# Parking a lane pair's results feature-major in DRAM, transposing them a quarter per unit in the next pair, and issuing the sync queue in hand-set order

## Chip, cores, metric

One core of one Trainium2 chip. The metric is the device time of the kernel in microseconds (us). All runs are single-core. A run is called "slow" when it is over 1.5% above the fastest run of the same kernel; ratios use the other ("fast") runs.

## The reference

A cross network of six layers on 16384 rows of 1024 features, all bf16:

```python
def reference(x0, ws, bs):          # x0 [16384,1024], ws [6,1024,1024], bs [6,1024]
    x = x0
    for l in range(6):
        proj = jnp.einsum('bd,de->be', x, ws[l]) + bs[l]
        x = x0 * proj + x
    return x
```

## The kernel before

The batch is cut into 8 *pairs* (`lp`) of two *lanes* of 1024 rows. Features lie on partitions, so an input is transposed on the way in and a result on the way out. A *unit* is one layer of one lane. Each 1024x1024 product is done by two levels of a seven-product scheme: TensorE runs a unit's 20 steps (`idx` 0 to 19), ScalarE (ACT) moves the sums out of PSUM, VectorE (DVE) adds them, multiplies by `x0` and adds `x`. All weights come back from DRAM (`Lc`) for each layer, nine loads of 512 KB per two units, through a ring of ten buffers: `wp<-Lc` in the profile. The parts that matter (`# ...` marks a cut):

```python
x0L = [res.tile([P, 2, KD, NB], BF16, ...) for i in range(2)]   # x0 of each lane, resident
xL  = [res.tile([P, 2, KD, NB], BF16, ...) for i in range(2)]   # x of each lane, resident
# ...
def pre_x0(lp, lane, eh, n):        # x0 of the next pair: transposed, then put aside in DRAM
    xs = late["xf"].tile([P, KH, KH, P], BF16, name="xf")            # two buffers
    nc.sync.dma_start_transpose(out=xs[:]..., in_=x0[r0:r0 + NB, eh * H:(eh + 1) * H])
    nc.sync.dma_start(x0s[lp % 2, lane, eh, n], xs[:]...)
def fetch_x0(lp, lane, eh, n):      # ... and fetched when the lane changes pairs
    nc.sync.dma_start(q(x0L[lane], eh, n)..., x0s[lp % 2, lane, eh, n])
def store_quarter(lp, lane, eh, n, xf):
    nc.sync.dma_start_transpose(out=dst, in_=xf[:]...)               # SBUF -> SBUF, into xL
    nc.sync.dma_start(out[r0:r0 + NB, ...], q(xL[lane], eh, n)...)
# ... in a unit:
P1s, Q2, U2s, S53, U3s, P5s = (ev_pool.tile(...) ...)                # bufs=1
def x_out(c, eh, n):                # c is Q2 (n = 0) or S53 (n = 1)
    if last_layer:
        xf = late["xf"].tile(...)
        tt(xf[:]..., c..., q(xst, eh, n)..., ADD)
        store_quarter(lp, lane, eh, n, xf)
    elif l > 0:
        nc.gpsimd.dma_start(q(xst, eh, n), c, accum_op=ADD)          # DMA that adds: xL += c
    else:
        tt(q(xst, eh, n), c, q(x0T, eh, n), ADD)
```

In layers 1 to 4 half of each unit's update is added by DMA from Q2 and S53 (`xL<-Q`, `xL<-S` on the POOL queue). I call these the Q and the S accumulate. In layer 5 VectorE adds into an `xf` buffer that is transposed and stored; in layer 0 VectorE adds as well. The scheduler decides the order of the sync queue (SP); the other engines follow program order.

## Time and profile before

| | |
|---|---|
| median of runs | 2375.8 us (2372.7 to 2377.8) |
| span of the profiled run | 2373.7 us |
| TensorE busy | 2264.8 us |
| one unit in the middle of a pair | 23.38 us |
| twelve such units | 280.6 us |
| pair to pair, five periods from 596.8 to 2058.5 | 292.3 us on average |

The page, lines of parts 1 and 2. Each digit is the busy share, or the clock granted to TensorE, of one fortieth of the span.

```profile
span 2373.7 us, 32873 instructions
PE 2264.8 (95%) x12659; PEld 1267.6 (53%) x12912; DVE 2114.4 (89%) x2096; ACT 1784.9 (75%) x2485; POOL 110.7 (5%) x133
...
PE   5999999999899998999989999999998999989996
...
PEclk9999999999999999999999999999999999999998
DMA  9876599546994579845798457975579656865566
```

TensorE dips every fifth digit or so, at the pair boundaries, where the DMA engines are full; between them the DMA share drops to 4 or 5 tenths. One boundary in the timeline of TensorE (start, duration, instruction; in brackets the idle time before it and what ended it):

```profile
617.23 0.60 PE L281 MATMUL XB<-t,wp 128*128 128x256 bf16 x4
622.41 1.04 PE L281 MATMUL XB<-ti,wp 128*128 128x256 bf16 x4 [4.59 <-DMA wp<-Lc]
623.24 1.91 PE L269 MATMUL XA<-t,wp 128*128 128x512 bf16 x4
...
628.68 1.03 PE L269 MATMUL XA<-x0L,wp 128*128 128x512 bf16 x4
```

TensorE waits 4.59 us for a weight load, and afterwards four matmuls take 1.91 us where they normally take 1.03. The windows of the same stretch (columns: window, its length, busy us and count of PE, PEld, DVE, ACT, POOL, granted clock, DMA share, GB/s; a packet's whole time is booked in the window in which it starts, so a share can pass 1):

```profile
616.00:620.00 4.00, 1.83 (x11) 0.81 (x9) 0.00 (x0) 1.17 (x3) 0.00 (x0) 1.00 1.17 250
620.00:624.00 4.00, 1.59 (x6) 0.89 (x7) 3.40 (x5) 0.51 (x1) 0.00 (x0) 0.55 0.91 320
624.00:628.00 4.00, 3.98 (x15) 1.95 (x15) 2.44 (x2) 2.20 (x3) 0.00 (x0) 0.60 1.04 404
628.00:632.00 4.00, 3.97 (x22) 2.13 (x22) 3.80 (x5) 3.15 (x5) 0.00 (x0) 1.00 1.20 252
```

Why the load is late shows in the timeline of the sync queue (here the duration is that of the issue):

```profile
611.74 0.98 SPq L171 DMA_DIRECT2D x0L<-x0s  x1
612.82 5.47 SPq L176 DMA_TRANSPOSE xL<-xf  x1
618.39 1.01 SPq L110 DMA_DIRECT2D wp<-Lc  x2
```

The two loads stand behind a transpose that holds the queue for 5.47 us. From the view of waits (total us, times, longest):

```profile
DVE xf L65 <- DMA xL<-xf: 59.5, 15, 6.3
PE XB L281 <- DMA wp<-Lc: 33.6, 13, 4.7
DVE t L65 <- DMA xL<-S: 28.5, 23, 2.4
...
ACT S L261 <- DMA xL<-S: 4.5, 6, 1.3
```

So the kernel is bound by TensorE's issue inside a pair, and loses 11 to 12 us (292.3 - 280.6) at each of seven boundaries.

### The profile page before, as it was taken

Reading aid. Unit: us, or ns where it says so; the run is one execution under the profiler, and the core shown is the slowest. Engines: PE = TensorE matmul, PEld = TensorE weight load, DVE = VectorE, ACT = ScalarE, POOL = GpSimd, SP = SyncE. Lnnn points to the kernel's source line nnn. Section 1 sums busy time; section 2 is a strip of 40 time slices with the busy share of each in tenths; the row PEclk is TensorE's granted clock in tenths of the full one; section 3 lists DMA queues with packets and bytes.
Section 4 is the critical chain, followed back from the end, with each engine's and each line's share of the span. In section 5 each row is a group of like instructions: output and inputs, shape, how many; then the busy total and the mean of one; then the engine's idle time right before and its main releaser. Section 6 shows DMA issues by size and latency. Waiting matters only on the chain.

```text
span 2373.7 us, 32873 instructions
## 1 busy us (share of the span) xinstructions
PE 2264.8 (95%) x12659; PEld 1267.6 (53%) x12912; DVE 2114.4 (89%) x2096; ACT 1784.9 (75%) x2485; POOL 110.7 (5%) x133
## 2 busy tenths in 40 slices
PE   5999999999899998999989999999998999989996
PEld 2555545555455554555545555555554555545553
DVE  5999879999898988999889998899988999889987
ACT  3777777777677776777867777677776777768775
POOL 0000000000000000000000000000000000000000
PEclk9999999999999999999999999999999999999998
DMA  9876599546994579845798457975579656865566
GB/s 274 236 231 216 159 285 252 156 126 179 290 254 128 134 189 291 247 121 138 189 300 229 124 150 201 299 202 133 156 208 303 183 140 167 219 187 133 150 171 142
DMA packets 410236, 468.27 MB, mean 197 GB/s; under 512 B 278496, under 2 KB 324064, under 8 KB 410080
## 3 DMA queue, kind: packets, MB, share of 16 engines
q1 hardware_dynamic: 391648, 399.05, 57.2%
q0 software_dynamic: 18432, 67.12, 14.8%
q8 instruction: 101, 1.65, 0.3%
q14 instruction: 55, 0.45, 0.1%
HBM read 240.65 MB, written 91.23 MB: 140 GB/s over the span
## 4 chain that ended last, share of the span: by engine, by line
PE 75%; DVE 15%; DMA 6%; issue 2%; ACT 1%; SPq 1%; DVEq 0%; ACTq 0%; POOLq 0%
PE pA L269 34%; PE XA L269 22%; PE XB L281 18%; DVE t L65 4%; DMA xL<-xf 4%; DVE D L65 3%; DVE ti L65 3%; DVE S L65 2%; DMA x0L<-x0s 1%; DVE xL L65 1%; DVE Q L65 1%; DVE xf L65 1%; SPq L161 0%; DMA xL<-S 0%; DMA wp<-Lc 0%
## 5 line engine op out<-in xcount | busy, mean ns | idle before, releaser
L269 PEld LDWEIGHTS <-wp 128*128 128x128 bf16 x7712 | 757.3, 98 | 757.0 <-issue 35.1
L269 PE MATMUL pA<-t,wp 128*128 128x512 bf16 x2982 | 758.7, 381 | 6.4
L281 PEld LDWEIGHTS <-wp 128*128 128x128 bf16 x5040 | 494.6, 98 | 311.2 <-DMA wp<-Lc 42.5
L261 ACT CAST F<-XB 128x1024 bf16<-128x1024 f32 x360 | 364.3, 1012 | 262.9 <-PE XB L281 256.5
L281 PE MATMUL XB<-ti,wp 128*128 128x256 bf16 x2880 | 435.1, 274 | 43.0 <-DMA wp<-Lc 33.2
L269 PE MATMUL XA<-t,wp 128*128 128x512 bf16 x1474 | 386.1, 385 | 3.7 <-DMA wp<-Lc 0.5
L269 PE MATMUL XA<-xL,wp 128*128 128x512 bf16 x1256 | 325.5, 379 | 4.0 <-ACT P5s L261 2.6
L269 PE MATMUL pA<-xL,wp 128*128 128x512 bf16 x1254 | 323.2, 379 | 1.3
L264 ACT ACTIVATE U3s<-pA,b_all 128x512 bf16<-128x512 f32 x384 | 264.4, 689 | 39.0 <-PE pA L269 19.0
L261 ACT CAST G<-XB 128x512 bf16<-128x512 f32 x360 | 212.0, 589 | 97.1 <-PE XB L281 95.8
L264 ACT ACTIVATE P1s<-pA,b_all 128x512 bf16<-128x512 f32 x384 | 266.4, 694 | 24.2 <-PE pA L269 16.5
L264 ACT ACTIVATE U2s<-pA,b_all 128x512 bf16<-128x512 f32 x384 | 266.5, 694 | 12.7 <-PE pA L269 4.2
L261 ACT CAST S<-XA 128x1024 bf16<-128x1024 f32 x192 | 194.3, 1012 | 66.6 <-PE XA L269 61.0
L65 DVE TENSOR_TENSOR D<-D,x0L 128x4096 bf16<-128x4096 bf16 x96 | 220.0, 2292 | 13.6 <-ACT D L264 10.1
L261 ACT CAST P5s<-XA 128x1024 bf16<-128x1024 f32 x192 | 195.1, 1016 | 44.4 <-DVE D L65 27.2
L65 DVE TENSOR_TENSOR t<-xL 128x4096 bf16<-128x4096 bf16 x80 | 183.4, 2293 | 41.6 <-DMA xL<-S 28.5
L65 DVE TENSOR_TENSOR t<-xL,t 128x2048 bf16<-128x2048 bf16 x160 | 194.9, 1218 | 0.0
L65 DVE TENSOR_TENSOR xL<-D,xL 128x4096 bf16<-128x4096 bf16 x64 | 146.7, 2292 | 7.0 <-DVE D L65 0.5
L327 POOL DMA_DIRECT2D xL<-Q x64 | 55.2, 862 | 1870.7 <-ACT U3s L264 948.5
L281 PE MATMUL XB<-t,wp 128*128 128x256 bf16 x1008 | 139.8, 276 | 0.0
L65 DVE TENSOR_TENSOR S<-S,U2s 128x2048 bf16<-128x2048 bf16 x96 | 117.2, 1221 | 24.0 <-ACT S L261 24.0
L65 DVE TENSOR_TENSOR Q<-Q,P1s 128x2048 bf16<-128x2048 bf16 x96 | 117.6, 1225 | 19.7 <-ACT Q L261 10.9
(43 smaller groups left out, 1744.0 us busy)
## 6 DMA issues: line engine op xcount, KB each, us to landing
wp<-Lc SPq DMA_DIRECT2D x378, 512.0 KB, 4.9
xL<-Q POOLq DMA_DIRECT2D x64, 512.0 KB, 6.2
xL<-S POOLq DMA_DIRECT2D x64, 512.0 KB, 6.8
out_dram<-xL SPq DMA_DIRECT2D x64, 512.0 KB, 4.1
x0s<-xf SPq DMA_DIRECT2D x56, 512.0 KB, 3.4
x0L<-x0s SPq DMA_DIRECT2D x56, 512.0 KB, 6.3
Lc<-wp SPq DMA_DIRECT2D x48, 512.0 KB, 4.7
wp<-in_ws_dram SPq DMA_DIRECT2D x13, 512.0 KB, 6.7
```

Source lines behind the costliest of these rows:

```text
L65: return nc.vector.tensor_tensor(out=out, in0=in0, in1=in1, op=op)
L261: nc.scalar.copy(out=dst, in_=src)
L264: nc.scalar.activation(out=dst, in_=src, func=IDENT, bias=bias_col(eh, m), scale=1.0)
L269: nc.tensor.matmul(dst, lhsT=w_[:, k, m * P:(m + 1) * P], rhs=b_[:, k, :], start=(start and k == 0), stop=(k == KH - 1), skip_group_check= ...
L281: nc.tensor.matmul(dst[:, m * NQ:(m + 1) * NQ], lhsT=wv[:, k, m * P:(m + 1) * P], rhs=b_[:, k, :], start=(start and m == 0 and k == 0), st ...
L327: nc.gpsimd.dma_start(q(xst, eh, n), c, accum_op=ADD)
```

## The change

Its intent is to take the output transposes out of the boundary. In layer 5 of all pairs but the last, results go into `xL` by the ordinary path (accumulates and one add), are *parked* as they are in DRAM (`outs`), and one quarter per unit is transposed and stored during layers 1 to 4 of the next pair, beside one quarter of the next x0. From the second pair on the sync queue is in program order, and `at(u, step, ...)` puts each transfer at a step of a unit. The diff, cut to its core:

```diff
+    def park_out(lp, lane, eh, n):
+        nc.sync.dma_start(outs[...].rearrange("(k r) b -> r k b", r=P), q(xL[lane], eh, n))
+    def post_out(lp, lane, eh, n):
+        xs = late["xf"].tile([P, KH, KH, P], BF16, name="xf")
+        nc.sync.dma_start_transpose(out=xs[:]..., in_=outs[lp % 2, lane, eh, n])
+        return lambda: nc.sync.dma_start(out[r0:r0 + NB, ...], xs[:]...)
...
+        if lp == 1 and sp_order is None:
+            sp_order = ctx.enter_context(tc.manual_schedule(engines={nc.sync.engine}))
...
-            if last_layer:
+            if direct:                       # last layer of the last pair only
...
                 nc.gpsimd.dma_start(q(xst, eh, n), c, accum_op=ADD)
+                if last_layer:
+                    at(u + n, 17 if n == 0 else 3, lambda: park_out(lp, lane, eh, n))
...
-        if 1 <= l <= 4 and lp + 1 < NLP:
-            pre_x0(lp + 1, i_ // 4, i_ % 2, (i_ // 2) % 2)
+        if 1 <= l <= 4:
+            if lp > 0:
+                at(u, 1, lambda u=u, a_=(lp - 1,) + qt: at(u, 7, post_out(*a_)))
+            if lp + 1 < NLP:
+                at(u, 9, lambda u=u, a_=(lp + 1,) + qt: at(u, 17, pre_x0(*a_)))
...
-                    fetch_x0(lp + 1, lane, 1, n)
+                    at(u + 1, 6, lambda n=n: fetch_x0(lp + 1, lane, 1, n))
...
+                        at(u + 1, 10, lambda n=n: park_out(lp, lane, 1, n))
```

## The prediction

> **What bounds the kernel now.** TensorE: 2264.8 of 2373.7 us busy (page, part 1). Within a lane pair it is issue-bound: in the chain of waits a unit (one layer of one lane) repeats every 23.38 us (412.73, 436.11, 459.49). Twelve units would take 280.6 us, but the seven pair-to-pair periods average about 291.5 us (596.83, 889.24, 1184.28, 1475.83 ...). So about 11 us is lost at each of 7 pair boundaries, about 77 us in all; start (25 us) and tail (18 us) are outside this.
>
> The timeline of 600 to 640 us shows the loss. TensorE waits 0.65, 1.04 and 4.59 us for weight loads (wp<-Lc), and after the 4.59 us its granted clock is 0.55 to 0.60 for about 6 us, about 4 us more. The loads are late because the sync queue is in order and stands behind xL<-xf transposes (3.7 us each to issue; they wait for VectorE), while VectorE waits for transposes to release xf buffers: 59.5 us in 15 waits. The Trainium skill, "TensorE: Matmul & The Clock Gate", Part 1, says an idle of about 3.4 us halves the clock; the trace agrees (1.04 us did not, 4.59 us did).
>
> **What changes, for 7 of 8 pairs.**
> - Removed at the boundary: 56 SBUF transposes, their xf waits, 56 xf adds (1.22 us each). In their place one 2.29 us add and two accumulate DMAs per unit: VectorE saves 2.6 us per last-layer unit, to 21.6 us, under TensorE's 23.38.
> - Added: 28 accumulates, 56 parking writes. The 56 output transposes move into layers 1 to 4 of the next pair, one per unit, beside one x0 transpose; those no longer bunch behind the boundary.
>
> **DMA load.** From the DMA queue shares: an accumulate takes 2.74 us of all 16 engines, a 512 KB load 1.53, a transpose about 3.1 (estimate: the rest of queue 1). Layers 1 to 4 then need 9x1.53+4x1.53+4x2.74+4x3.1 = 43 us per 46.8 us (92%). Critical is the S accumulate: from t's start to the next S issue VectorE takes 14.2 us, so two consecutive latencies must stay under 46.8-28.4 = 18.4 us. Now they are 4.5 (before lane 1) and 8.5 to 9.6 (before lane 0, beside weight loads). A transpose issued at step 1 falls on it; accumulates beside transposes in the first pair took 5.9. I estimate 6 to 7 plus 10 to 11.5: just inside; 0 to 15 us lost in all, probably 4.
>
> **Boundary afterwards.** Weights no longer stand behind waits of consequence. VectorE runs late instead: the x0 fetch at step 6 waits behind a park that waits for the S accumulate, and layer 0 needs 24.0 us of VectorE; through ACT P5s this costs TensorE an estimated 2 to 3 us, too short for the clock to fall. At the very end transposes and stores alternate in program order: about +2.5 us.
>
> **Time.** 2375.8 - 77 + 7x2.5 + 4 + 2.5 = about 2322; I say 2321 us, 2302 to 2345. Chances: faster 0.64, same 0.34, slower 0.02.
>
> **What would show it.** TensorE's waits for wp<-Lc fall from 33.6 us to under 8; DVE xf waits to near none; clock dips at boundaries gone; pair periods about 283 us; DMA share flat near 0.8 to 0.9 instead of 1.1 and 0.4; "t <- DMA xL<-S" rises above 28.5 us.
>
> **What would make it wrong.** S accumulates above 18.4 us per two: every unit of layers 1 to 4 grows and the gain is eaten. Weights late in layers 1 to 4 behind transposes in program order. VectorE late enough for 4 us idles, so that the clock falls again. Better: a free boundary, 2300.

## The result

2344.6 us (2341.4 to 2350.1) against 2375.8: a ratio of 0.987 (0.985 to 0.990). Ratios are the mean time of one kernel's fast runs over that of the other's of the same rounds, so not quite the ratio of the medians quoted. The traced execution below is the slowest of the four (2350.1), so its stalls may be longer than usual. By the 2% rule that is "same"; by the interval it is a gain of 1.3%. I had given "faster by over 2%" a chance of 0.64, and the time lies at the very edge of my range.

The page after:

```profile
span 2348.4 us, 33208 instructions
PE 2269.0 (97%) x12912; PEld 1265.8 (54%) x12912; DVE 2079.6 (89%) x2054; ACT 1780.7 (76%) x2485; POOL 134.7 (6%) x161
...
PE   5999999999999999999999999999999999998996
...
PEclk9999999999999999999999999999999999999998
DMA  9877577998789987898868888689985899847876
```

The dips at the boundaries are gone and the DMA share is flat, at 7 to 9 tenths. But one digit of TensorE, near the end, is 8 where no boundary dip had been. The view of waits:

```profile
DVE t L66 <- DMA xL<-S: 63.0, 21, 8.4
...
ACT S L289 <- DMA xL<-S: 39.1, 18, 7.3
...
PE XA L297 <- ACT S L289: 18.5, 13, 6.0
DVE t L66 <- DMA x0L<-x0s: 15.7, 10, 3.4
...
PE XA L297 <- ACT P5s L289: 11.4, 12, 1.9
...
PE XB L309 <- DMA wp<-Lc: 0.7, 1, 0.7
```

TensorE's wait for weights went from 33.6 to 0.7 us and the `xf` wait of VectorE is off the list. In their place stands a chain that was harmless before: the S accumulate lands late, ACT cannot refill the single S buffer, and TensorE finds its PSUM bank XA full (18.5 us). The longest case, in the windows:

```profile
2139.00:2143.00 4.00, 2.97 (x16) 1.47 (x15) 0.00 (x0) 0.57 (x1) 0.00 (x0) 1.00 1.19 60
2143.00:2147.00 4.00, 0.00 (x0) 0.00 (x0) 0.08 (x1) 0.12 (x1) 0.00 (x0) 0.96 1.21 76
2147.00:2151.00 4.00, 3.06 (x11) 1.55 (x11) 3.93 (x5) 2.54 (x4) 0.00 (x0) 0.50 0.59 158
2151.00:2155.00 4.00, 4.00 (x20) 2.03 (x19) 3.86 (x5) 2.71 (x3) 0.00 (x0) 0.69 0.51 108
```

and in the sync queue and the DMA view (issues in the window from 2131 us, with us to landing):

```profile
2130.68 10.14 SPq L181 DMA_TRANSPOSE xf<-outs  x1
```

```profile
xL<-S POOLq DMA_DIRECT2D x1, 512.0 KB, 15.7
xf<-outs SPq DMA_TRANSPOSE x1, 17.1
```

The packets of the two queues from 2143 to 2147 us (number, MB, share of 16 engines; q1 carries what the sync queue issues, q0 what the POOL queue issues):

```profile
q1 hardware_dynamic: 1028, 0.26, 115.5%
q0 software_dynamic: 12, 0.04, 5.5%
```

An output transpose and an S accumulate are in flight together. For 8 us the DMA share is as high as at the boundary before (1.19 and 1.21), but the engines move only 60 and 76 GB/s. In the second window the only transfer of q1 in flight is the transpose, and its packets are nearly all of that share. Both transfers take some three and a half times the shortest of their kind in this trace (4.5 us for an S accumulate, 4.7 for an output transpose). TensorE stands still and then runs at half clock, as at the old boundaries.

The stall can be read off the latency. S accumulates that follow a lane-0 unit land in 4.7 us (median; before 4.5), those that follow a lane-1 unit in 10.7, at most 15.7 (before 9.05, at most 10.3). The first of these after each boundary, with the stall of TensorE for ACT S that follows it:

| S accumulate, us to landing | 10.5 | 10.7 | 10.7 | 11.1 | 12.6 | 12.7 | 15.7 |
|---|---|---|---|---|---|---|---|
| TensorE's stall, us | 0.76 | 1.04 | 0.97 | 1.39 | 2.87 | 2.94 | 5.96 |

In every column the stall is the latency less 9.7 to 9.8 us. These seven are 15.9 of the 18.5 us. The other six stalls follow later accumulates of a pair, and there the same difference is 10.8 us (11.6 us to landing, a stall of 0.78). The other measured differences: five pair periods now average 287.1 us (from the stalls at 630.6 to 2066.0), and the tail, from the start of the last `xf` add to the end, is 15.9 us (before 12.4).

### The profile page after: what moved, and what is told of

Read it like the earlier page. It is cut to its first block, busy times and chain, and to the rows that moved or that the text cites. A ratio compares the mean times of both kernels' runs of the same rounds, so it can differ in the third digit from the quotient of the medians.

```text
span 2348.4 us, 33208 instructions
## 1 busy us (share of the span) xinstructions
PE 2269.0 (97%) x12912; PEld 1265.8 (54%) x12912; DVE 2079.6 (89%) x2054; ACT 1780.7 (76%) x2485; POOL 134.7 (6%) x161
## 5 line engine op out<-in xcount | busy, mean ns | idle before, releaser
L297 PE MATMUL pA<-t,wp 128*128 128x512 bf16 x3104 | 774.4, 379 | 0.0
L297 PE MATMUL XA<-t,wp 128*128 128x512 bf16 x1536 | 396.7, 382 | 18.6 <-ACT S L289 18.5
L297 PE MATMUL pA<-xL,wp 128*128 128x512 bf16 x1280 | 328.6, 379 | 0.0
L66 DVE TENSOR_TENSOR D<-D,x0L 128x4096 bf16<-128x4096 bf16 x96 | 220.0, 2292 | 15.0 <-ACT D L292 11.5
L66 DVE TENSOR_TENSOR xL<-D,xL 128x4096 bf16<-128x4096 bf16 x78 | 178.8, 2292 | 8.1
L357 POOL DMA_DIRECT2D xL<-Q x78 | 67.2, 862 | 1743.5 <-ACT U3s L292 494.4
L66 DVE TENSOR_TENSOR Q<-Q,P1s 128x2048 bf16<-128x2048 bf16 x96 | 117.7, 1226 | 29.6 <-ACT Q L289 21.3
```

The source lines that it names most:

```text
L66: return nc.vector.tensor_tensor(out=out, in0=in0, in1=in1, op=op)
L297: nc.tensor.matmul(dst, lhsT=w_[:, k, m * P:(m + 1) * P], rhs=b_[:, k, :], start=(start and k == 0), stop=(k == KH - 1), skip_group_check= ...
```

## Experiments

The S latencies quoted are medians and maxima of the accumulates after lane-1 units of layers 1 to 4, from the second pair on, read from each kernel's trace. In the runs e9_free, e10_noT, e12_noS and e6_fetch the trace is of another execution than the timed ones, 2 to 9 us apart.

| run | what | median (range), us | ratio to before | S after lane 1 |
|---|---|---|---|---|
| (before) | | 2375.8 (2372.7-2377.8) | 1 | 9.05, max 10.3 |
| (changed) | | 2344.6 (2341.4-2350.1) | 0.987 | 10.7, max 15.7 |
| e1_plain | output transposes replaced by plain loads | 2330.1 (2326.9-2332.5) | 0.980 | 10.05, max 11.8 |
| e2_late | transposes at steps 8 and 13 | 2358.4 (2331.4-2369.0) | 0.988 | 8.5, max 13.7 |
| e3_s2 | two S buffers | 2342.3 (2333.8-2357.3) | 0.986 | 10.7, max 11.5 |
| e4_order | kernel before, hand order only | 2455.6 (2446.7-2472.8) | 1.032 | 9.3, max 19.2 |
| e5_noorder | parking, scheduler's order | 2444.4 (2440.1-2449.0) | 1.029 | 8.85, max 10.3 |
| e6_fetch | x0 fetch ahead of the park | 2336.8 (2334.2-2338.0) | 0.983 | 10.35, max 14.6 |
| e9_free | transposes away from accumulates | 2338.4 (2334.5-2340.3) | 0.984 | 9.85, max 11.2 |
| e10_noT | no steady transposes | 2331.6 (2329.5-2332.9) | 0.981 | 9.85, max 12.7 |
| e12_noS | no S accumulates | 2321.7 (one run) | | |
| e13_hold | weight loads held back | 2393.6 (2361.0-2413.3) | 0.999 | 10.65, max 25.8 |
| e14_holdplain | the same, plain loads | 2319.8 (2316.0-2321.1) | 0.976 | 10.0, max 11.3 |
| b3 | hold + free + fetch + tail | 2321.9 (2316.9-2325.4) | 0.977 | 10.2, max 14.5 |
| b5 | hold + fetch + tail | 2393.3 (2370.3-2413.8) | 1.004 | 10.65, max 25.5 |
| b7 | other places, held | 2334.6 (2331.3-2342.7) | 0.983 | 9.95, max 16.9 |
| b8 | other places, not held | 2348.1 (2332.3-2355.2) | 0.987 | 9.8, max 19.4 |

Slow runs: one of four of e2_late, three of six of e13_hold, two of six of b5. The outputs of e1_plain, e10_noT and e14_holdplain are wrong on purpose. That of e12_noS lacks a term too, and still passed the comparison: with these inputs the missing increments lie inside its tolerance.

### The two halves alone

e4_order is the kernel before with nothing but this:

```diff
+        if lp == 1 and sp_order is None:
+            sp_order = ctx.enter_context(tc.manual_schedule(engines={nc.sync.engine}))
```

> The kernel before with nothing but the sync queue in program order from the second pair on. If the hand-set order alone were the gain: about 2350. My theory is that parking is the gain, as program order leaves weight loads behind transposes that wait for VectorE and stores that wait for transposes: 2375 or slower, up to 2420, TensorE's waits for wp<-Lc above 33.6 us.

e5_noorder is the changed kernel with those lines taken out.

> The changed kernel without the hand-set order of the sync queue (the scheduler's order, parking kept). If parking alone is the gain, within 6 us of 2345. If the order is needed with it (weight loads behind parks that wait for accumulates): 2360 or more, TensorE's waits for wp<-Lc above 10 us.

Order alone costs 3.2%, parking alone costs 2.9%, together they gain 1.3%. The waits of e4_order, then of e5_noorder:

```profile
DVE xf L65 <- DMA xL<-xf: 99.5, 21, 11.5
PE XB L284 <- DMA wp<-Lc: 62.9, 19, 6.4
```

```profile
PE XB L307 <- DMA wp<-Lc: 71.7, 21, 13.1
```

With the old store path, program order makes every store wait on the queue for its transpose, and weights wait behind. With parking but the scheduler's order, weight loads stand behind a run of transposes that now have nothing else to wait for: six waits, one per pair, are 61.7 of the 71.7 us. One of them in the sync queue of e5_noorder; TensorE waits until 726.2 us for the first of the nine loads:

```profile
710.84 5.43 SPq L168 DMA_TRANSPOSE xf<-in_x_dram  x1
...
721.45 5.10 SPq L111 DMA_DIRECT2D wp<-Lc  x9
```

Both expectations held in direction; e4_order came out above the range I gave, e5_noorder far above its threshold. Neither half is the gain.

### Is it the transpose or the load?

e1_plain replaces the output transpose by a plain load of the same bytes at the same step.

```diff
-        nc.sync.dma_start_transpose(out=xs[:].rearrange("p a b r -> p a (b r)"), in_=outs[...])
+        nc.sync.dma_start(xs[:].rearrange("p a b r -> p a (b r)"), outs[...].rearrange("(a p) c -> p a c", p=P))
```

> The 56 output transposes at step 1 are replaced by plain loads of the same 512 KB (the output is wrong on purpose). Theory A (a transpose beside an accumulate slows both, in the changed kernel 0.5 MB moved at 20 to 40 GB/s while the S accumulate took 11 to 15.7 us): S accumulates of lane 1 fall from 10-12.7 us to 8.5-9.6, TensorE's wait for ACT S from 18.5 us to under 4, time about 2325. Rival B (any extra half megabyte behind the weight loads delays the accumulate, DMA load is what counts): latencies stay 10 us and more, time within 5 us of 2345.

```profile
ACT S L289 <- DMA xL<-S: 21.6, 19, 2.4
...
PE XA L297 <- ACT P5s L289: 12.8, 10, 2.6
...
PE XA L297 <- ACT S L289: 3.1, 5, 1.1
```

2330 us, about 15 less than the changed kernel, and the stalls on ACT S fall from 18.5 to 3.1 us. So most of the harm is in the transpose, not in the 512 KB. But the median latency fell only to 10.05 us, not to the 8.5 to 9.6 I expected: the transpose mostly makes the long tail, and the added load explains some of the median. And the late landing of these transfers is mostly their place: in lane-0 units (the first of a pair left out) the plain loads took 11.3 us (median) and the transposes 11.8. e10_noT replaces the x0 transposes as well:

> Output and x0 transposes of the steady part all replaced by plain copies of the same size and place (wrong output on purpose). Theory A, if x0 transposes at step 9 also meet accumulates: a little faster than with the output transposes alone replaced (2330), about 2322 to 2328, spread under 6 us, S accumulates of lane 1 9 us. Rival B: 2345; or no change from 2330, then the x0 transposes are harmless where they stand.

2331.6 us: nothing beyond e1_plain. Where they stand, at step 9, the x0 transposes cost nothing that these runs show. A long accumulate does not need a transpose, though: one here took 12.7 us beside a plain load, and TensorE stood 3.0 us for it. This pair also prices a transpose. The queue's share of 16 engines is 62.0% of 2348.4 us in the changed kernel and 54.6% of 2334.6 here, with the same bytes: (1456.0 - 1274.7) / 112 = 1.6 us more per transpose than per plain copy of the same size. That is the price in company, where packets also wait. Alone in flight, at the start of the kernels, an x0 transpose (at 55.6 us in the trace before) landed in 4.2 us with 2.4 us of all engines' time, a plain load of the same bytes (at 54.9 us in e10_noT) in 3.5 us with 1.6.

### What the S accumulate costs in all

e12_noS leaves the S accumulates of layers 1 to 4 out.

```diff
-                nc.gpsimd.dma_start(q(xst, eh, n), c, accum_op=ADD)
+                if n == 0 or lp == 0 or last_layer:
+                    nc.gpsimd.dma_start(q(xst, eh, n), c, accum_op=ADD)
```

> The S accumulates of layers 1 to 4 from the second pair on are left out (wrong output on purpose), transposes stay at step 1. Theory A (mutual: the transpose is slow because of the accumulate): output transposes in lane-0 units land in 5 to 7 us instead of 11 to 17. Rival B2 (the transpose is slow because it stands behind three weight loads): still 10 us and more. The time falls too, as VectorE and ACT no longer wait for S: 2310 to 2320.

2321.7 us, in one run: the S accumulates, their DMA load included, cost the changed kernel about 23 us (20 to 28 against its four runs), of which about 15 go when the transposes beside them become plain loads. In the trace TensorE waits nowhere for ACT S, while its waits for ACT P5s stay as they were (11.5 us, 11.4 in the changed kernel). So in these two traces what TensorE lost to the S accumulates came through the S buffer, and not through VectorE's 63.0 us of waits. The output transposes in lane-0 units (the first of a pair, which meets no accumulate, left out) took 9.4 us to landing (median; 7.0 to 12.6) instead of 11.8 (10.6 to 17.1). They are slow partly because of the accumulate, but not as purely as I expected (5 to 7): the weight loads ahead of them have a share.

### The single S buffer

```diff
+    s_pool = ctx.enter_context(tc.tile_pool(name="sp2", bufs=2))
+        S53 = s_pool.tile([P, KH, NB], BF16, name="S53")
```

> A second S53 buffer, transposes left at step 1. Theory C (the long accumulate hurts through the single S53 buffer: ACT cannot write S until the accumulate has read it): ACT's waits for DMA xL<-S (39.1 us) vanish and TensorE's wait for ACT S (18.5 us) falls under 4, S latencies stay at 10-12.7; time about 2325. If instead VectorE's lateness (t waits for xL<-S, 63 us) is what costs, the stall moves to ACT P5s or DVE t and the time stays within 6 us of 2345.

```profile
DVE t L67 <- DMA xL<-S: 66.6, 20, 3.8
```

In the profiled run, the fastest at 2333.8 us, ACT's wait for `xL<-S` is gone and TensorE waits nowhere for ACT S; VectorE still waits 66.6 us for the S accumulates, and weights cost TensorE 10.8 us again. The other runs are 2337 to 2357, so the mean (2343.9) is that of the changed kernel (2345.1). The buffer is where the stall shows, but a second one did not bring the expected 20 us; what its slower runs wait for is not known, as none of them was traced.

### Moving the transposes

e2_late only moves the output transposes to step 8 (store 12) and those of x0 to step 13 (store 18).

> Output transposes moved from step 1 to step 8 (store 12), x0 transposes from 9 to 13 (store 18): same work, other place. Theory A (collision with the S accumulate at the unit's start): S accumulates of lane 1 back at 8.5-9.6 us, DVE t waits for xL<-S from 63 to about 30 us, TensorE's wait for ACT S under 4 us, time about 2322. Rival B (total DMA load of 92% in layers 1 to 4): no change beyond 5 us.

The latency fell to 8.5 us as expected and one run was 2331, but the others were 2352 to 2369: a long S accumulate (13.7 at most) still meets the transpose at step 8 in some executions. As a mean, a miss. e9_free puts them where the trace shows no accumulate under way:

```diff
+        if l == 0 and lp > 0:                       # layer 0 has no accumulates
+            turn(7, 11, post_out, (lp - 1, 0, 0, lane)); turn(12, 16, post_out, (lp - 1, 0, 1, lane))
+        if 1 <= l <= 4:
+            if lp > 0 and lane == 1: turn(5, 9, post_out, ...)
+            if lp + 1 < NLP: turn(10, 15, pre_x0, ...)
```

> All 112 transposes of the steady part kept, but issued only where by the trace no accumulate is in flight: four output quarters in layer 0 (which has none), four at step 5 of lane-1 units, x0 quarters at step 10, all else as in the changed kernel. Theory A (transpose beside accumulate): S accumulates of lane 1 at 8.5-9.6 us, no transpose over 9 us to landing, TensorE's wait for ACT S under 3 us, time 2322 to 2330 and the spread between runs under 8 us (the run that only moved them to step 8 spread over 38 us). Rival B (DMA load): as the changed kernel, 2345.

2338.4 us: the spread (6 us) as expected, the gain, also 6 us, well short of the 15 to 23 expected. The stalls on ACT S fell from 18.5 to 4.9 us in its trace, but not all transposes became short: the x0 transposes of one lane took 12 to 14 us.

### The boundary

e6_fetch puts the x0 fetch at step 4 and the S park behind it, at step 9.

```diff
-                    at(u + n, 17 if n == 0 else 3, lambda: park_out(lp, lane, eh, n))
+                    at(u + n, 17 if n == 0 else 9, lambda: park_out(lp, lane, eh, n))
-                    at(u + 1, 6, lambda n=n: fetch_x0(lp + 1, lane, 1, n))
+                    at(u + 1, 4, lambda n=n: fetch_x0(lp + 1, lane, 1, n))
```

> At the boundary the x0 fetch goes to step 4 and the S park behind it to step 9, so the fetch no longer stands behind a park that waits for the S accumulate. If that order is why VectorE is late there: t waits for x0L<-x0s fall from 15.7 us to under 4, TensorE's waits for ACT P5s from 11.4 to about 4, time 8 to 14 us less, about 2334. If the lateness is layer 0's own VectorE work (24.0 us a unit): x0L waits fall, P5s waits stay near 10, time within 5 us of 2345.

```profile
PE XA L297 <- ACT S L289: 13.7, 14, 4.9
...
DVE t L66 <- DMA x0L<-x0s: 13.0, 6, 2.5
...
PE XA L297 <- ACT P5s L289: 5.9, 12, 0.7
```

2336.8 us, about 8 less. The P5s stalls halve (11.4 to 5.9), though VectorE's wait for the fetch hardly falls in total. Part of the boundary lateness is the order of fetch and park.

### Holding weight loads back

Three weight loads are freed at the end of each lane-1 unit, just before its S accumulate. e13_hold keeps two of them until step 7 of the next unit, to give the accumulate room.

```diff
-                prefetch()
+                prefetch(99 if lp == 0 or idx < 18 else 1 if idx == 18 else 0)
...
+        if lp > 0 and lane == 0 and u > 12:
+            at(u, 7, prefetch)
```

> The changed kernel with two of the three weight loads at the end of each lane-1 unit held back to step 7 of the next unit (they are needed at step 16 and a layer later). Leaving the S accumulates out gave 2322, so their cost is about 23 us; if the weight loads beside them are a main part: S accumulates of lane 1 fall from 10-12.7 to 6-8 us, TensorE's wait for ACT S from 18.5 to under 5, time 2325 to 2332. If the transpose beside them alone matters: latency stays above 9.5, time within 5 us of 2345.

b5 is the same with the earlier fetch and, at the end, the last two stores after both last transposes:

> As b3 but transposes at steps 1 and 9 as in the changed kernel. If holding the weight loads back is enough, 2315 as b3; if the transpose at step 1 still lengthens the S accumulate, 5 to 12 us slower than b3.

Both lost the whole gain of the change, and against my expectation: the three fast runs of e13_hold are 2361.0, 2370.5 and 2387.1 us. Its profiled run, a slow one, has S accumulates of up to 25.8 us. My reading: with the loads out of the way the transpose reaches the DMA engines right beside the accumulate instead of behind the loads. It was tested by e14_holdplain: e13_hold with plain loads for the output transposes.

> e13_hold (weight loads held back, which made it slower: 2361 to 2413, S accumulates up to 25.8 us) with the output transposes at step 1 replaced by plain loads of the same size (wrong output on purpose). If a transpose in flight with the accumulate is the cause: S accumulates of lane 1 fall to 6.5-9 us, none over 12, TensorE's wait for ACT S under 4 us, time about 2322 to 2328, spread under 8 us. If holding the loads back is itself harmful: still over 2350.

e13_hold, in its slow run, and then e14_holdplain:

```profile
PE XA L298 <- ACT S L290: 72.8, 13, 15.0
```

```profile
ACT S L290 <- DMA xL<-S: 21.5, 17, 2.9
...
DVE t L66 <- DMA x0L<-x0s: 7.6, 7, 1.9
PE XA L298 <- ACT S L290: 4.4, 6, 1.6
...
PE XA L298 <- ACT P5s L290: 0.4, 2, 0.2
```

2319.8 us with a spread of 5 us. One edit, transpose to plain load, takes 54 us off the mean of e13_hold's fast runs (2372.9 to 2319.2), and no S accumulate is over 11.3 us. That settles what makes the very long ones of e13_hold: the transposes at step 1. The median latency stayed at 10.0 us, but that does not clear the weight loads, because holding them to step 7 did not keep them away. Here the held loads are issued up to 2.2 us after the S accumulate (at 741.6 us, the accumulate at 740.7); in e13_hold they come behind the transpose's issue, 4 to 10 us after it. The number of weight loads in flight during one of these accumulates is 3.8 on average before, 4.1 in the changed kernel and 4.1 here. So e13_hold did not give the accumulate the room that it was meant to. What holding does is at the boundary: the fetch comes sooner (VectorE waits 7.6 us for it, 20.0 in e1_plain) and the P5s stalls vanish (12.8 us in e1_plain, 0.4 here).

### Combinations

b3 is e13_hold, e9_free and e6_fetch together, with the last two stores after both last transposes.

> Combination: weight loads held back, transposes where e9_free put them, x0 fetch ahead of the park, last two stores after both last transposes. If the parts add (23 us for S, 8 for the fetch, 2 to 4 at the tail): 2312, range 2305 to 2325.

```profile
PE XA L301 <- ACT S L293: 12.5, 10, 4.8
...
PE XA L301 <- ACT P5s L293: 0.4, 2, 0.2
```

2321.9 us, a correct kernel and faster than both: 2.3% under the kernel before, 1% under the changed one. Its tail is 12.7 us from the start of the last `xf` adds, 15.9 in the changed kernel. Against b5 it shows again that holding loads back pays only where no transpose takes their place. The parts did not add up to the 2312 expected: stalls on ACT S of 12.5 us remain.

b7 and b8 were to keep transposes clear of the S accumulates after lane-1 units altogether: both x0 transposes in lane-0 units, at steps 8 and 11, the output transpose at step 6 of lane-1 units; b8 without the held loads.

> As b3, but in layers 1 to 4 both x0 transposes in lane-0 units (steps 8 and 11) and only the output transpose in lane-1 units (step 6), so that none is still under way when a lane-1 S accumulate starts. S accumulates of lane 1 7 to 9 us instead of 9 to 11, TensorE's wait for ACT S under 4 us: 2308 to 2315 against 2322 of b3. If these accumulates are long for the total DMA load: 2322 as b3.

> As b7 but with the three weight loads left where they were. If transposes alone count: as b7 within 4 us. If the weight loads beside the S accumulate cost too: S accumulates of lane 1 9 us and more, 4 to 10 us slower than b7.

Both missed. The longest S accumulates (16.9 and 19.4 us) are now the first after a boundary: they meet the transpose at step 8, where b3 has it at step 10. Held loads are worth 10 to 14 us between the two (by the ratios and by the medians; the ranges overlap), at an equal median latency (9.95 and 9.8). Why the S accumulates after lane-1 units stay near 10 us, while those after lane-0 units take 4.5, no run tests. The traces show one difference: three to five weight loads are in flight during each of the former, in the kernel before and in e14_holdplain alike, and mostly none during the latter. An estimate comes near: four loads of 1.53 us and the accumulate's own 2.74 are 8.9 us of all engines, against a latency of 9.05 before, though part of those loads has moved when the accumulate is issued. No run kept the loads away.

## Why the prediction was right or wrong

- **"about 11 us is lost at each of 7 pair boundaries", through weight loads behind transposes.** Right. The waits for weights fell from 33.6 to 0.7 us, the `xf` waits vanished, the boundary dips of TensorE too.
- **"this costs TensorE an estimated 2 to 3 us" at the boundary through ACT P5s.** Right for the mechanism, and nearly for the size: 11.4 us of stalls over six boundaries, 1.9 each, and e6_fetch shows the named order of fetch and park to be part of it.
- **"too short for the clock to fall" and "clock dips at boundaries gone".** True of the boundary stalls of this trace (1.9 us at most). But it was near the edge: in e1_plain P5s stalls of 2.58 and 1.91 us, ending at 1199.5 and 1771.5 us, were each followed by a clock of 0.50 (1199.6 to 1203.0 and 1773.0 to 1776.4). And in the changed kernel the dips came back elsewhere, after the S stalls: 0.50 and 0.69 in the windows above.
- **Latencies "6 to 7 plus 10 to 11.5".** Close: medians of 4.7 and 10.7 us. What I did not foresee is the tail, 12.6, 12.7 and 15.7 us.
- **The step that failed: "two consecutive latencies must stay under 46.8-28.4 = 18.4 us ... just inside; 0 to 15 us lost in all, probably 4".** It measured about 23 us (e12_noS, one run). The criterion was the wrong one. I followed only VectorE's loop through `t`. The same accumulate reads the only S buffer, and ACT must refill it at a fixed place in the next unit: by the seven stalls the limit is a single latency of about 9.8 us for the first accumulate of a pair after a lane-1 unit, and by the other six 10.8 us for the later ones. Before, these first accumulates stood at 8.5 to 9.6 us, just under it, with ACT already waiting 4.5 us for them. A pair of 4.6 and 12.6 us sums to 17.2, inside my limit, and stalls TensorE 2.9 us. That the loss goes this way is read from the traces of the changed kernel and of e12_noS; that a second buffer pays is not shown, as e3_s2 took the stall away and kept the mean. And I costed the transposes by their engine time, as added load. In e1_plain and e14_holdplain plain loads of the same bytes took 15 and 54 us less. Some of that is the longer engine time of a transpose; that there is more to it is seen from 2143 to 2147 us, where the transpose took 4.6 us of all engines (115.5% of 4 us) for 0.26 MB, while an x0 transpose of 0.52 MB alone in flight takes 2.4.
- **Where the transposes stood.** Before, they were bunched around the boundary: in the one shown they were issued from 574.3 to 678.5 us, and no accumulate was issued between 555.8 and 680.6. I read the bunching as the fault to be mended. It also kept transposes and accumulates apart, and the change spread the transposes over exactly the layers that have accumulates.
- **The end, "about +2.5 us".** It was +3.5 (12.4 to 15.9 us).
- **Sum.** My terms without the S term were 2375.8 - 77 + 17.5 + 2.5 = 2318.8; the changed kernel without S accumulates took 2321.7. The S term, 4 predicted and 23 measured, is nearly all of the miss of 23.6 us.

The Trainium skill was used twice. "DMA: Bandwidth & Descriptors", section "Issuing engines are not separate DMA queues", says that transfers from all queues run on the same 16 engines and interleave; the trace agrees, as the accumulates on the POOL queue lengthen with what the sync queue carries (in the kernel before 4.5 us mostly alone, 9.05 us beside weight loads). "TensorE: Matmul & The Clock Gate", Part 1, gives idle windows of about 3.4 us, free-running, for the clock to fall. This case agrees in kind, with shorter idles. In the changed kernel a stall of 1.88 us kept the clock at 1.00, while 2.94 us (ending at 995.0) was followed by 0.51 from 996.4 to 999.8. Over all traces there is no sharp limit: 1.76 us in e3_s2 (ending at 2058.2) was followed by 0.50 from 2059.5 to 2062.9, and 2.19 us in the kernel before (ending at 1229.6) by 1.00.

## What to carry to other kernels

When you spread a burst of transfers to flatten the DMA load, look at what else is in flight in the places they go to, not only at the sum: here an accumulating DMA of 4.5 us took 9 beside weight loads, and up to 15.7 with a transpose added. For each transfer find every consumer, including the one that waits to overwrite its source, and measure how far each stands from its limit; one at 9.6 of 9.8 us has no room for anything new. Look also at the spread of the runs: the kernels with plain loads in the place of transposes varied by 3 to 6 us, those with output transposes at steps 1 or 8 of layers 1 to 4 by 4 to 52.

## What the Trainium skill lacked or had wrong

- "DMA: Bandwidth & Descriptors", "Rules for kernel authors", says that a transpose next to ordinary DMAs needs nothing. For the result that held here. For time it lacks the case of a transpose next to an accumulating DMA: 60 and 76 GB/s with the engines busy, 15.7 us for an accumulate that takes 4.5 alone, and 54 us between the fast runs of e13_hold and e14_holdplain.
- "Advanced Engine Details and Errata", "X-Bar Transpose (TRN2)", says that transpose DMAs are as fast as regular ones, and expects about 90% of a copy's bandwidth. Here a 512 KB transpose alone in flight landed in 4.2 us with 2.4 us of all engines' time (before), a plain load of the same bytes in 3.5 us with 1.6 (e10_noT). In company the difference was 1.6 us of all engines (e10_noT against the changed kernel), against 1.53 us for a 512 KB load in the trace before (29.6% of the 140 us from 700 to 840 us, over 27 loads).
- "TensorE: Matmul & The Clock Gate", Part 1: the clock fell after idles of 2.94 us (the changed kernel) and 1.76 us (e3_s2), shorter than the page's window of about 3.4 us.
- No page gives the time of an accumulating DMA within a core: 2.74 us of all engines' time for 512 KB, SBUF to SBUF, in the trace before (14.8% of 2373.7 us over 128 of them).
